# Attention with an MLP gate on one core: matmul sums in the mixer's second stage, first token transposes ahead of K and V, and a drain with a PSUM bank for each piece of Wo

## Chip, cores and metric

The kernel runs on one core of a Trainium2 chip. The metric is the device time of one execution in microseconds (us), the median of several runs. The profile is that of one execution, and its times are microseconds from the first instruction of the program.

## What is computed

```python
x = A_x                       # 2048 tokens, D = 512
xn = _layernorm(x)
# A: attention over a cache; 32 heads of 128, 2048 keys and values each
q = (xn @ wq) as 32 heads
p = softmax(q @ k_cache^T * 128 ** -0.5)
s = (p @ v_cache) @ wo
# B: a mixer and an MLP on the same xn
h  = gelu(_layernorm(xn) @ w1)                 # 512 -> 512
hs = (four column groups of h, shifted by +1, -1, +2, -2 tokens) @ w2
x1 = xn + hs
h2 = gelu(_layernorm(x1) @ w3) @ w4            # 512 -> 1792 -> 512
g = silu(x1 + h2)
return x + s * g
```

All inputs and the output are bf16.

## The kernel before

The attention is cut into 128 units. A unit is one head and one block of 512 queries; units run over 8 groups of 4 heads, in each group over 4 query blocks, and in each block over the 4 heads. A unit has 8 slots (`SPU`), and slot `n` of the whole program is unit `n // 8`, place `p = n % 8`. In a slot TensorE makes two score matmuls (keys by queries, 128x512 each) into a tile of two PSUM banks (`ps_s`, two buffers), and ScalarE turns them with one Exp into half of a `pT` tile. The value matmuls of a slot (`pv_slot`) run some slots after its scores; that distance is `lag`, 5 at first, up to 10 through most of the program, and 5 again at its end. The list `LAGS` says from which slot on which lag holds.

The denominators of a unit's softmax come from adding its four `pT` tiles on DVE (`add_first`, `add_next`) into `acc`, folding `acc` twice (`fold`), and summing over the 128 key partitions. For the last step there are two forms. In the first (`sums`) four matmuls of one column against a vector of ones write a [128, 4] tile in PSUM. In the second (`acc_turn`, `turned_sums`) a DMA transpose on SP's queue turns `acc`, and DVE reduces the turned tile along its free dimension. `turned(u)` chooses: units from `T0` up to `T1` use the second form. Either way DVE takes the reciprocals (`recip`), a DMA writes them to DRAM (`dr`), another one reads them back to all partitions (`rb`, in `bcast`), and DVE multiplies the unit's output by them (`norm`) on its way out of PSUM into `oT`. Unit `u` has these steps in the slots of the units after it:

| step | matmul sums | turned sums |
|---|---|---|
| last add, `fold` | unit u+1, places 0, 0 | unit u+1, places 0, 2 |
| sum over partitions | u+1, place 3 | u+1, place 3 (turn), u+2, place 0 (reduce) |
| `bcast` | u+1, place 4 | u+2, place 2 |
| `norm` | u+2, place 2 | u+2, place 7 |

The queries of unit `u + 2` are computed in places 0 and 1 of unit `u` (`q_mm`) and copied to SBUF in place 2 (`q_copy`), by DVE or by ScalarE. The product with Wo of a finished query block is made in places 4 and 5, one tile of 128 tokens for each unit (`wo_mm`), and added to `s_acc` in place 6 (`wo_post`). PSUM has eight banks: four for `ps_s`, two for the outputs `ps_o`, and one each for the tags `xa` (queries, sums, Wo) and `xm` (mixer and MLP).

The mixer and the MLP are cut into 136 chunks, and a planner lays them evenly over the units from the fifth to the 120th, at places 2, 3 and 6, 7. The chunks of the mixer's first matmul with its Gelu come first (units 5 to 18), those of its second one next (units 18 to 31, `m2_chunk`: a normalisation, a sum out of PSUM and token statistics on DVE for each), and those of the MLP after that. `w3_prefetch` loads the MLP's weights on GpSimd's queue.

Other work hangs on slots through `at(n, ...)`. `tokens` says in which slots the token tiles 4 to 15 get their statistics, their normalisation and their DMA transpose into `xnT` (on SP's queue); below it stand the slots of the loads of K, V and Wo for the first group, on the same queue. Work of one slot is issued in the order in which it was put there. Tiles 0 to 3 are turned on TensorE at the very start (`first_tokens`), since the first unit waits for them.

After the last slot comes the drain (L849 to L896): the value matmuls and sums of the last unit, then the product with Wo for the last four token tiles (`ts`, tiles 12 to 15). Each of these is the sum of a part for the last but one head group (`GL - 1`, held back) and one for the last group (`GL`). `last_scale` multiplies it by half the gate in `gf`, `last_out` adds the rest (prepared in `s_acc`) and stores the tile.

`pin` keeps an engine's instructions in the order of the program. All matmuls are issued through the helper on L115.

Of the kernel before, what the change touches and what calls it, by code (L numbers as in the profile page):

```python
# [17 lines left out]
def kernel(  # L18
# [95 lines left out]
    def mm(out, lhsT, rhs, start, stop):  # L114
        pin(nc.tensor.matmul(out=out, lhsT=lhsT, rhs=rhs, start=start, stop=stop))  # L115
# [11 lines left out]
    NS = NU * SPU  # L127
    T0, T1 = 3 * HG, NU - 10
    M2 = (18, 31)
    LAGS = [((T0 - 2) * SPU + 4 * (i + 1), LAG + i) for i in range(5)] + [((T1 + 2) * SPU + 2, LAG + 5)]  # L130
    LAGS += [((T1 + 2) * SPU + 6 + 4 * i, LAG + 4 - i) for i in range(4)] + [(NS, LAG)]
# [48 lines left out]
    def q_copy(u):  # L180
        qT = qtp.tile([P, 512], BF16, name="qT")
        if u > QUIET + 1 or M2[0] <= u - 2 <= M2[1]:
            pin(nc.scalar.activation(out=qT[:], in_=st[u].pop("psq")[:], func=ACT.Identity))
        else:
            pin(nc.vector.tensor_copy(out=qT[:], in_=st[u].pop("psq")[:]))  # L185
        st[u]["qT"] = qT
# [111 lines left out]

    def wo_part(ps, g, t, hhs, first, last):
        oT = oTs[(g, t // 4)]  # L300
        ts = t % 4
        for hh in hhs:
            mm(ps, oT[:, hh, ts * P:(ts + 1) * P], wos[g * HG + hh][:],
               first and hh == hhs[0], last and hh == hhs[-1])
# [22 lines left out]

    def last_scale(t, ps):
        gf, xf = tl[t]
        pin(nc.vector.scalar_tensor_tensor(  # L330
            out=gf[:], in0=ps, scalar=0.5, in1=gf[:], op0=ALU.mult, op1=ALU.mult))

    def last_out(t, eng):
        gf, xf = tl.pop(t)
        pin(eng.tensor_tensor(out=xf[:], in0=gf[:], in1=s_acc[:, t, :], op=ALU.add))
        pin(nc.sync.dma_start(out=out2d[t * P:(t + 1) * P, :], in_=xf[:]))

# [88 lines left out]
    def first_tokens():  # L426
# [18 lines left out]

        def back(t, eng, cs=slice(0, DC)):
            dst, src = xnT[:, cs, t * P:(t + 1) * P], tps[t][:, cs, :]
            if eng == "V":
# [8 lines left out]

        lo, hi = slice(0, DC // 2), slice(DC // 2, DC)
        turn(0)
# [6 lines left out]
        turn(3)  # L466
        for t in (2, 3):
            back(t, "A", lo)
            back(t, "V", hi)
        pin(nc.scalar.activation(out=qT[:, 0:2 * P], in_=qA[:, 0:2 * P], func=ACT.Identity))  # L470
# [255 lines left out]
    for t, (stats, apply, turn) in enumerate(tokens, 4):  # L726
# [4 lines left out]
        at(turn, lambda t=t: ln1_turn(t))  # L731
    for n, h, piece in ((2, 2, 2), (4, 2, 3), (12, 3, 0), (15, 3, 1), (19, 3, 2), (20, 3, 3)):
        at(n, lambda h=h, piece=piece: load_k(h, (piece,)))
    for n, h, half in ((7, 2, 0), (13, 2, 1), (20, 3, 0), (21, 3, 1)):
        at(n, lambda h=h, half=half: load_v(h, (half,)))
    at(28, ph1_load)
    at(64, w2_load)
    for h in range(HG):
        at(31 + h, lambda h=h: load_wo(h))
    for g in range(NG - 1):  # L740
# [137 lines left out]
    pc = psX.tile([P, D], FP32, tag="xa", name="ps_wo")  # L878
    dst = [pa[:, 0, :], pa[:, 1, :], pb[:, 0, :], pc[:]]
    for j in (0, 1):  # L880
        wo_part(dst[j], GL - 1, ts[j], held, True, False)
        wo_part(dst[j], GL, ts[j], ready, False, False)
    for j in (2, 3):
        wo_part(dst[j], GL - 1, ts[j], held, True, False)
    norm(U, 2)
    for j in (0, 1):
        wo_part(dst[j], GL, ts[j], (HG - 1,), False, True)
    for j in (2, 3):
        wo_part(dst[j], GL, ts[j], range(HG), False, True)
    for j in range(4):  # L890
        last_scale(ts[j], dst[j])
        if j < 2:
            last_out(ts[j], nc.gpsimd)
    for j in (2, 3):
        last_out(ts[j], nc.vector)
    ph.close()  # L896
# [30 lines left out]
```

## Time and profile before

| what | value |
|---|---|
| median of three runs | 1271.95 us (1271.66 to 1273.48) |
| the profiled execution | 1272.68 us |
| its span, first to last instruction | 1270.9 us |
| granted TensorE clock, mean | 0.999 |
| TensorE matmuls busy | 1254.7 us (99%) |
| DVE, ScalarE busy | 1099.7 us (87%), 1118.5 us (88%) |

The profile names its engines PE (TensorE matmuls), PEld (TensorE weight loads), DVE (VectorE), ACT (ScalarE), POOL (GpSimd) and SP (SyncE, which issues DMAs; SPq is its queue). In a timeline a row has its start, its length, engine, source line and operation, output and inputs, and how many instructions it merges; idle time of the engine before it stands in brackets with what ended it. In a table of groups the bar is followed by busy time and mean nanoseconds, and then by the idle time before the group. In a table of stretches each engine has its busy time and its count; the last three numbers are the granted clock, the DMA engines' busy share and GB/s. Matmuls are pipelined: a row's length includes a part that the next matmul overlaps.

### The profile page before, as it was taken

The numbers are of one execution on the slowest core, as the hardware profiler recorded it, in microseconds if no ns is written. First come the engines' busy times: TensorE is split into PE (matmuls) and PEld (weight loads), VectorE is DVE, ScalarE is ACT, GpSimd is POOL, SyncE is SP. The second block draws the span as 40 slices with busy tenths as digits, with TensorE's granted clock in tenths as the row PEclk, the third lists the DMA queues.
The fourth block names the chain that finished last, engine by engine and source line by source line (L and its number), as shares of the span: only waits on it lengthen the run. The fifth ranks groups of instructions, "written<-read, shape, count | busy, mean of one in ns | idle before, by whom it ended". The sixth has DMA issues, their size and how long they took to land.

```text
span 1270.9 us, 16580 instructions
## 1 busy us (share of the span) xinstructions
PE 1254.7 (99%) x5896; PEld 598.5 (47%) x5896; DVE 1099.7 (87%) x1499; ACT 1118.5 (88%) x1215; POOL 140.8 (11%) x239
## 2 busy tenths in 40 slices
PE   9999999999999999999999999999999999999998
PEld 5444444444444444444444444444444444444444
DVE  7888889998899888888898888989888899888886
ACT  8899998887999988899998889998888999988893
POOL 4420003333110010000000000000000000000111
PEclk9999999999999999999999999999999999999999
DMA  9533354466744465244454344435545344463532
GB/s 178 142 88 72 60 111 99 101 141 117 133 96 95 109 116 109 54 90 103 89 111 84 78 98 98 104 66 96 105 93 110 63 81 87 102 127 50 152 78 67
DMA packets 230612, 125.65 MB, mean 99 GB/s; under 512 B 182464, under 2 KB 207552, under 8 KB 230528
## 3 DMA queue, kind: packets, MB, share of 16 engines
q1 hardware_dynamic: 221568, 99.41, 39.9%
q0 software_dynamic: 8672, 24.91, 8.2%
q8 instruction: 46, 0.75, 0.3%
q14 instruction: 38, 0.31, 0.1%
q10 hardware_dynamic: 288, 0.26, 0.1%
HBM read 82.58 MB, written 7.60 MB: 71 GB/s over the span
## 4 chain that ended last, share of the span: by engine, by line
PE 70%; ACT 12%; DVE 11%; DMA 4%; issue 2%; POOL 0%; SPq 0%; DVEq 0%; POOLq 0%
PE ps_s L115 26%; PE ps_o L115 25%; ACT pT L199 9%; PE ps_m L115 7%; PE ps_wo L115 6%; PE ps_q L115 6%; DVE acc L210 4%; ACT pre L515 1%; DVE oT L279 1%; DMA rb<-dr 1%; ACT sq L485 1%; DVE sm L252 1%; ACT sq L494 1%; DVE acc L214 1%; DMA dr<-rc 1%
## 5 line engine op out<-in xcount | busy, mean ns | idle before, releaser
L199 ACT ACTIVATE pT<-ps_s 128x1024 bf16<-128x1024 f32 x1024 | 1013.5, 1033 | 129.5 <-PE ps_s L115 121.7
L115 PE MATMUL ps_s<-qT,kT 128*128 128x512 bf16 x2048 | 608.5, 379 | 2.8 <-ACT pT L199 0.8
L115 PE MATMUL ps_o<-pT,vb 128*128 128x512 bf16 x2048 | 607.7, 379 | 2.2 <-DVE oT L279 1.9
L115 PEld LDWEIGHTS <-kT 128*128 128x128 bf16 x2048 | 230.7, 113 | 237.4 <-issue 24.7
L210 DVE TENSOR_TENSOR acc<-acc,pT 128x2048 bf16<-128x2048 bf16 x254 | 307.1, 1209 | 18.1 <-ACT pT L199 17.1
L115 PEld LDWEIGHTS <-vb 128*128 128x128 bf16 x2048 | 199.6, 98 | 228.0 <-issue 3.3
L205 DVE TENSOR_TENSOR acc<-pT 128x2048 bf16<-128x2048 bf16 x128 | 156.1, 1219 | 24.0 <-ACT pT L199 23.4
L115 PE MATMUL ps_q<-xnT,wq_h 128*128 128x512 bf16 (+1 forms) x524 | 152.3, 374 | 2.5 <-DVE s_acc L353 1.1
L115 PE MATMUL ps_wo<-wo_h,oT 128*128 128x512 bf16 x468 | 138.9, 379 | 0.3 <-DVE rc L237 0.3
L279 DVE TENSOR_TENSOR oT<-ps_o,rb 128x512 bf16<-128x512 f32 x106 | 113.7, 1073 | 8.9 <-DMA rb<-dr 8.9
L353 DVE TENSOR_TENSOR s_acc<-ps_wo,s_acc 128x512 f32<-128x512 f32 x100 | 68.9, 689 | 52.5 <-PE ps_wo L115 52.4
L214 DVE TENSOR_TENSOR acc<-acc 128x1024 bf16<-128x1024 bf16 x127 | 87.0, 685 | 1.2
L185 DVE CAST qT<-ps_q 128x512 bf16<-128x512 f32 x108 | 74.1, 686 | 14.5 <-PE ps_q L115 14.5
L115 PEld LDWEIGHTS <-wq_h 128*128 128x128 bf16 x524 | 50.7, 98 | 63.6 <-issue 2.8
L252 DVE TENSOR_REDUCE sm<-accT 128x4 f32<-128x512 bf16 x106 | 72.2, 681 | 2.8 <-DMA accT<-acc 2.8
L115 PEld LDWEIGHTS <-oT 128*128 128x128 bf16 x480 | 46.9, 98 | 57.4 <-issue 1.1
L115 PE MATMUL ps_m<-xn2T,w_sb 128*128 128x512 bf16 x224 | 66.6, 379 | 0.0
L115 PE MATMUL ps_m<-w_sb,h2T 128*128 128x512 bf16 x224 | 64.0, 379 | 0.0
L640 POOL DMA_DIRECT2D w_sb<-in_B_w_dram x28 | 21.2, 758 | 361.8 <-PE ps_m L115 327.0
L215 DVE TENSOR_TENSOR acc<-acc 128x512 bf16<-128x512 bf16 x127 | 54.0, 425 | 4.4
L489 DVE SCALAR_TENSOR_TENSOR sq<-sq,pre 128x1024 bf16<-128x1024 bf16 x36 | 43.9, 1219 | 0.0
L515 ACT ACTIVATE pre<-ps_m 128x512 bf16<-128x512 f32 x72 | 42.7, 593 | 1.1 <-PE ps_m L115 1.1
(89 smaller groups left out, 559.2 us busy)
## 6 DMA issues: line engine op xcount, KB each, us to landing
rb<-dr SPq DMA_DIRECT2D x128, 256.0 KB, 4.2
vb<-in_A_v_cache_dram SPq DMA_DIRECT2D x64, 256.0 KB, 3.5
w_sb<-in_B_w_dram POOLq DMA_DIRECT2D x28, 256.0 KB, 4.3
wo_h<-in_A_wo_dram SPq DMA_DIRECT2D x32, 128.0 KB, 3.2
wq_h<-in_A_wq_dram SPq DMA_DIRECT2D x28, 128.0 KB, 3.1
kT<-in_A_k_cache_dram SPq DMA_TRANSPOSE x128, 3.5
dr<-rc SPq DMA_DIRECT2D x128, 2.0 KB, 1.6
xr<-in_A_x_dram POOLq DMA_DIRECT2D x16, 128.0 KB, 2.7
```

The source lines that it names most:

```text
L115: pin(nc.tensor.matmul(out=out, lhsT=lhsT, rhs=rhs, start=start, stop=stop))
L185: pin(nc.vector.tensor_copy(out=qT[:], in_=st[u].pop("psq")[:]))
L199: pin(nc.scalar.activation(out=s["pT"][-1][:, jj:jj + 2, :], in_=sps[:], func=ACT.Exp, scale=SCALE))
L205: pin(nc.vector.tensor_tensor(out=s["acc"][:], in0=s["pT"][0][:], in1=s["pT"][1][:], op=ALU.add))
L210: pin(nc.vector.tensor_tensor(out=a[:], in0=a[:], in1=st[u]["pT"][i][:], op=ALU.add))
L214: pin(nc.vector.tensor_tensor(out=a[:, 0:2, :], in0=a[:, 0:2, :], in1=a[:, 2:4, :], op=ALU.add))
L215: pin(nc.vector.tensor_tensor(out=a[:, 0, :], in0=a[:, 0, :], in1=a[:, 1, :], op=ALU.add))
L252: pin(nc.vector.tensor_reduce(out=sm[:], in_=s.pop("at")[:], axis=mybir.AxisListType.X, op=ALU.add))
L279: pin(nc.vector.tensor_tensor(out=oTs[(g, qt)][:, hh, :].rearrange(f, j=4), in0=s["o"].rearrange(f, j=4), in1=s["rb"].rearrange("x (p j) - ...
L353: pin(nc.vector.tensor_tensor(out=sa, in0=ps[:], in1=sa, op=ALU.add))
L489: pin(nc.vector.scalar_tensor_tensor(out=sq[:].rearrange(f2), in0=sq[:].rearrange(f2), scalar=1.0, in1=pre[:].rearrange(f2), op0=ALU.add, ...
L515: pin(nc.scalar.activation(out=pre[:, j, :], in_=mlp["ps"][:], func=ACT.Identity))
```

## The change

There are three parts. (1) `T0` goes from 12 to 32, so units 12 to 31 take matmul sums in place of turned ones; the slots at which the lag rises move with it, to start in unit 32 in place of unit 10; and the queries of units 20 to 33 are copied by DVE again, not by ScalarE. (2) In the loads for the first group, pieces of K of the fourth head (and one half of V of the third) and the Wo tiles move to later slots, which puts the transposes of token tiles 6 and 7 ahead of them; in `first_tokens` tiles 2 and 3 are each copied whole by one engine. (3) In the drain, the first three token tiles get a PSUM tile of their own each, and each is scaled and put out as soon as its last matmul is issued. The fourth one is cut into two halves of 256 columns, each with its own PSUM bank, its own matmuls for both head groups, its own scaling, add and store, the second store on ScalarE's queue.

```diff
-    T0, T1 = 3 * HG, NU - 10
-    M2 = (18, 31)
-    LAGS = [((T0 - 2) * SPU + 4 * (i + 1), LAG + i) for i in range(5)] + [((T1 + 2) * SPU + 2, LAG + 5)]
+    T0, T1 = 8 * HG, NU - 10
+    LAGS = [(T0 * SPU + 4 * (i + 1), LAG + i) for i in range(5)] + [((T1 + 2) * SPU + 2, LAG + 5)]
...
-        if u > QUIET + 1 or M2[0] <= u - 2 <= M2[1]:
+        if u > QUIET + 1:
             pin(nc.scalar.activation(out=qT[:], in_=st[u].pop("psq")[:], func=ACT.Identity))
...
-    def wo_part(ps, g, t, hhs, first, last):
+    def wo_part(ps, g, t, hhs, first, last, cs=slice(0, D)):
...
-            mm(ps, oT[:, hh, ts * P:(ts + 1) * P], wos[g * HG + hh][:],
+            mm(ps, oT[:, hh, ts * P:(ts + 1) * P], wos[g * HG + hh][:, cs],
...
-    def last_scale(t, ps):
+    def last_scale(t, ps, cs=slice(0, D)):
         gf, xf = tl[t]
         pin(nc.vector.scalar_tensor_tensor(
-            out=gf[:], in0=ps, scalar=0.5, in1=gf[:], op0=ALU.mult, op1=ALU.mult))
-
-    def last_out(t, eng):
-        gf, xf = tl.pop(t)
-        pin(eng.tensor_tensor(out=xf[:], in0=gf[:], in1=s_acc[:, t, :], op=ALU.add))
-        pin(nc.sync.dma_start(out=out2d[t * P:(t + 1) * P, :], in_=xf[:]))
+            out=gf[:, cs], in0=ps, scalar=0.5, in1=gf[:, cs], op0=ALU.mult, op1=ALU.mult))
+
+    def last_out(t, eng, cs=slice(0, D), queue=nc.sync):
+        gf, xf = tl[t]
+        pin(eng.tensor_tensor(out=xf[:, cs], in0=gf[:, cs], in1=s_acc[:, t, cs], op=ALU.add))
+        pin(queue.dma_start(out=out2d[t * P:(t + 1) * P, cs], in_=xf[:, cs]))
...
-        def back(t, eng, cs=slice(0, DC)):
-            dst, src = xnT[:, cs, t * P:(t + 1) * P], tps[t][:, cs, :]
+        def back(t, eng):
+            dst, src = xnT[:, :, t * P:(t + 1) * P], tps[t]
...
-        for t in (2, 3):
-            back(t, "A", lo)
-            back(t, "V", hi)
+        back(2, "A")
+        back(3, "V")
...
-    for n, h, piece in ((2, 2, 2), (4, 2, 3), (12, 3, 0), (15, 3, 1), (19, 3, 2), (20, 3, 3)):
+    for n, h, piece in ((2, 2, 2), (4, 2, 3), (15, 3, 0), (16, 3, 1), (19, 3, 2), (20, 3, 3)):
         at(n, lambda h=h, piece=piece: load_k(h, (piece,)))
-    for n, h, half in ((7, 2, 0), (13, 2, 1), (20, 3, 0), (21, 3, 1)):
+    for n, h, half in ((7, 2, 0), (15, 2, 1), (20, 3, 0), (21, 3, 1)):
         at(n, lambda h=h, half=half: load_v(h, (half,)))
...
-        at(31 + h, lambda h=h: load_wo(h))
+        at((34, 35, 37, 38)[h], lambda h=h: load_wo(h))
...
-    dst = [pa[:, 0, :], pa[:, 1, :], pb[:, 0, :], pc[:]]
+    dst = [pa[:, 0, :], pb[:, 0, :], pc[:]]
+    halves = [psX.tile([P, D], FP32, tag="xm", name="ps_wo"), psO.tile([P, D], FP32, tag="ps_o", name="ps_wo")]
     for j in (0, 1):
         wo_part(dst[j], GL - 1, ts[j], held, True, False)
         wo_part(dst[j], GL, ts[j], ready, False, False)
-    for j in (2, 3):
-        wo_part(dst[j], GL - 1, ts[j], held, True, False)
+    wo_part(dst[2], GL - 1, ts[2], held, True, False)
     norm(U, 2)
     for j in (0, 1):
         wo_part(dst[j], GL, ts[j], (HG - 1,), False, True)
-    for j in (2, 3):
-        wo_part(dst[j], GL, ts[j], range(HG), False, True)
-    for j in range(4):
         last_scale(ts[j], dst[j])
-        if j < 2:
-            last_out(ts[j], nc.gpsimd)
-    for j in (2, 3):
-        last_out(ts[j], nc.vector)
+        last_out(ts[j], nc.gpsimd)
+    wo_part(dst[2], GL, ts[2], range(HG), False, True)
+    last_scale(ts[2], dst[2])
+    last_out(ts[2], nc.vector)
+    for i, queue in enumerate((nc.sync, nc.scalar)):
+        cs = slice(i * D // 2, (i + 1) * D // 2)
+        ps = halves[i][:, cs]
+        wo_part(ps, GL - 1, ts[3], held, True, False, cs)
+        wo_part(ps, GL, ts[3], range(HG), False, True, cs)
+        last_scale(ts[3], ps, cs)
+        last_out(ts[3], nc.vector, cs, queue)
```

More of the change, by code (lines that the diff above doesn't have):

```diff
@@ L456, in q_part @@
                 mm(psq[:, ts], wqs[0][:, dc, :], xnT[:, dc, ts], dc == 0, dc == DC - 1)
-        lo, hi = slice(0, DC // 2), slice(DC // 2, DC)
         turn(0)
```

## The prediction

> **What bounds the kernel now.** I read the page first, then stretches of the span cut at the first score matmul of a unit (one head of one query block: 8 slots, each with two score matmuls, one Exp and two value matmuls).
>
> ```profile
> span 1270.9 us, 16580 instructions
> PE 1254.7 (99%) x5896; PEld 598.5 (47%) x5896; DVE 1099.7 (87%) x1499; ACT 1118.5 (88%) x1215; POOL 140.8 (11%) x239
> ```
>
> TensorE is busy nearly always, so a change pays only where it removes TensorE work or a place where TensorE stands still. The stretches show where that is:
>
> ```profile
> 82.86:92.70 9.84, 9.84 (x50) 4.69 (x48) 8.24 (x13) 9.84 (x13) 2.74 (x4) 1.00 0.60 153
> 102.54:131.67 29.13, 28.29 (x140) 13.42 (x138) 24.67 (x32) 27.73 (x31) 0.00 (x0) 1.00 0.43 74
> 131.67:141.44 9.77, 9.71 (x46) 4.56 (x45) 7.44 (x9) 9.77 (x13) 0.00 (x0) 1.00 0.22 48
> 190.09:319.71 129.62, 126.62 (x581) 59.86 (x580) 119.25 (x186) 109.20 (x118) 44.94 (x77) 1.00 0.53 115
> 277.99:287.57 9.58, 9.58 (x45) 4.53 (x44) 8.78 (x14) 8.36 (x10) 5.13 (x8) 1.00 0.78 182
> 287.57:298.24 10.67, 9.66 (x46) 4.54 (x45) 5.38 (x9) 8.58 (x10) 1.45 (x3) 1.00 0.63 112
> 298.24:310.06 11.82, 9.86 (x46) 4.55 (x44) 11.51 (x19) 8.06 (x10) 6.17 (x10) 1.00 0.71 127
> ```
>
> Columns: stretch, length, then busy time and count of PE, weight loads, DVE, ACT, POOL. The lines are unit 8 (matmul sums, lag 5), units 10 to 12 (lag going from 5 to 10), unit 13 (turned sums, lag 10), units 19 to 31 (the mixer's second stage), and of these units 28, 29 and 30. Units 28, 29 and 30 have the same matmuls, yet 29 is 1.09 us and 30 is 2.24 us longer than 28. That is 3.3 us of standing TensorE in the stretch that the change rewrites. What stood in the way:
>
> ```profile
> 286.25 1.67 POOL L640 DMA_DIRECT2D w_sb<-in_B_w_dram  x2
> 286.46 0.34 SPq L269 DMA_DIRECT2D rb<-dr  x1
> 286.90 1.22 SPq L247 DMA_TRANSPOSE accT<-acc  x1
> 290.65 1.05 DVE L279 TENSOR_TENSOR oT<-ps_o,rb 128x512 bf16<-128x512 f32 x1 [2.19 <-DMA rb<-dr]
> 294.55 0.69 DVE L252 TENSOR_REDUCE sm<-accT 128x4 f32<-128x512 bf16 x1 [2.84 <-DMA accT<-acc]
> 300.33 0.59 PE L115 MATMUL ps_q<-xnT,wq_h 128*128 128x512 bf16 x2 [1.07 <-DVE s_acc L353]
> 303.55 0.59 PE L115 MATMUL ps_o<-pT,vb 128*128 128x512 bf16 x2 [0.89 <-DVE oT L279]
> ```
>
> Two loads of 256 KB for the MLP start on POOL at 286.25; the turn of `acc` issued at 286.90 is read only at 294.55, 7.6 us later. DVE waits 2.84 us for it, all behind it on DVE is late, and TensorE then waits for DVE twice.
>
> **Part 1, matmul sums for units 12 to 31.** It removes 20 DMA turns and 20 reduces, so the wait at 294.55 has nothing left to wait for: **-3.3 us**. Kept from below: if DVE comes just as late through `rb`, nothing is won (rival B). It adds 20 times four one-column matmuls. Their price:
>
> ```profile
> 1247.88 0.27 PE L115 MATMUL ps_sum<-ones_t,acc 128*128 128x1 bf16 x4
> 1248.01 0.60 PE L115 MATMUL ps_s<-qT,kT 128*128 128x512 bf16 x2
> ```
>
> The next score pair starts 0.13 us after the sums. Unit 8 against unit 13 gives 0.07 (ScalarE has its say in that stage). I take 0.13 for the 15 units from 17 on and 0.07 for five: **+2.3 us**, bounds 1.4 to 2.6.
>
> On DVE:
>
> ```profile
> L210 DVE TENSOR_TENSOR acc<-acc,pT 128x2048 bf16<-128x2048 bf16 x27 | 32.6, 1207 | 0.6 <-ACT pT L199 0.6
> L568 DVE SCALAR_TENSOR_TENSOR xr<-ps_m,xr 128x512 bf16<-128x512 f32 x16 | 11.0, 687 | 1.5 <-PE ps_m L115 1.0
> L214 DVE TENSOR_TENSOR acc<-acc 128x1024 bf16<-128x1024 bf16 x13 | 9.0, 692 | 0.4
> L252 DVE TENSOR_REDUCE sm<-accT 128x4 f32<-128x512 bf16 x13 | 8.9, 683 | 2.8 <-DMA accT<-acc 2.8
> L215 DVE TENSOR_TENSOR acc<-acc 128x512 bf16<-128x512 bf16 x13 | 5.5, 425 | 0.4
> L183 ACT ACTIVATE qT<-ps_q 128x512 bf16<-128x512 f32 x13 | 7.7, 592 | 0.0
> ```
>
> ```profile
> L279 DVE TENSOR_TENSOR oT<-ps_o,rb 128x512 bf16<-128x512 f32 x106 | 113.7, 1073 | 8.9 <-DMA rb<-dr 8.9
> L185 DVE CAST qT<-ps_q 128x512 bf16<-128x512 f32 x108 | 74.1, 686 | 14.5 <-PE ps_q L115 14.5
> L286 DVE TENSOR_TENSOR oT<-ps_o,rb 128x512 bf16<-128x512 f32 x21 | 14.4, 684 | 4.1 <-DMA rb<-dr 4.1
> ```
>
> Per unit DVE loses a reduce (0.68) and the slow form of the normalisation (1.07 becomes 0.68), and in 14 units takes over the q copy (0.69) from ScalarE (0.59). Net -0.4 us per unit, from 119.25 busy in 129.62 us, so DVE has a little more room. ScalarE gets more too. Units 19 to 31 hold 580 wide matmuls. What one costs from start to start comes from the page:
>
> ```profile
> L115 PE MATMUL ps_s<-qT,kT 128*128 128x512 bf16 x2048 | 608.5, 379 | 2.8 <-ACT pT L199 0.8
> ```
>
> They run in 1024 pairs of 0.594 us (608.5 over 1024), and the second alone takes 0.379, so it starts 0.215 after the first; with the rounding, 0.216. 580 of them are 125.3 of the 129.62 us, 3.3 of the rest are the stall above, and 1.0 is small waits. With ScalarE lighter I take off two thirds: **-0.7 us**, bounds -1.0 and 0.
>
> The new wait: TensorE, in order, may not pass the sums at slot 3 before DVE has folded `acc` and copied q out of the same PSUM tag. Behind it stand all score and value matmuls. From unit start to the sums are three slots of 1.22 us and a fourth's matmuls (0.87): 4.5 us. DVE, in the worst order, does in that time an L568 left over from slot 7 (0.69), the last add (1.21), both folds (0.69 and 0.43) and the copy (0.69): 3.7 us. So 0.8 us is spare when DVE enters the unit on time; where two mixer chunks fall in one unit it may not. I allow **+0.4 us** in all, bounds 0 and 3 (beyond that is rival A).
>
> The rise of the lag from 5 to 10 moves from units 10 to 12 to units 32 to 34. Ten value matmuls are put off there (2.2 us), but ScalarE can't follow: the line counts 126 wide matmuls beside 12 sums and two that reach in from outside, so with the ten there would be 136, which is three units like unit 8 and four matmuls, 30.4 us. Less 2.2 that is 28.2, and the line says 29.13, so the rise costs 0.9 us. Units 32 to 34 open the MLP's Gelu stage with a like load on ScalarE: I take the same there, **0**, bounds -0.9 and +1.0.
>
> **Part 2, transposes of tokens 6 and 7 ahead of pieces of K and V.**
>
> ```profile
> 26.01 1.15 SPq L151 DMA_TRANSPOSE kT<-in_A_k_cache_dram  x1
> 28.51 0.58 SPq L161 DMA_DIRECT2D vb<-in_A_v_cache_dram  x1
> 29.19 1.20 SPq L419 DMA_TRANSPOSE xnT<-xn  x1
> 33.49 0.61 PE L115 MATMUL ps_q<-xnT,wq_h 128*128 128x512 bf16 x2 [0.92 <-DMA xnT<-xn]
> 57.42 0.27 PE L115 MATMUL ps_sum<-ones_t,acc 128*128 128x1 bf16 x4 [0.98 <-DVE qT L185]
> ```
>
> SP issues in order. A piece of K (1.15) and one of V (0.58) go ahead of the transpose that TensorE waits for; moved behind, that transpose is issued about 1.8 us earlier, and the transfers it no longer follows are out of its way. The wait (0.92, about 1.1 from start to start) goes: **-1.1 us**, with -1.5 as the other bound if `rb` of unit 0 gains as well. Late next would be that piece of K. It is issued near 28.5, and the transpose issued at 29.19 ended TensorE's wait at 33.49, 4.3 us on, so the piece lands near 33. Unit 3 wants it: two slots after the q matmuls (four score, two value and two q matmuls, 1.7 us), which then come at 32.4, so near 34.1. That cover is about 1 us; if it is gone, the gain is 0. The Wo loads move behind a 2 KB and a 256 KB transfer; the wait at 57.42 is for DVE: **0**.
>
> **Part 3, the first tokens.**
>
> ```profile
> 8.89 0.87 DVE L449 CAST xnT<-ps_s 128x256 bf16<-128x256 f32 x2 [0.48 <-ACT xnT L451]
> ```
>
> DVE's two halves waited 0.48 for ScalarE's half of the same PSUM tile and end at 9.76. A whole copy from 8.9 takes 0.69 (L185), so it ends at 9.6, and then four small matmuls follow instead of two. **0**, bounds -0.2 and +0.2.
>
> **Part 4, the drain.**
>
> ```profile
> 1263.77 1.89 DVE L330 SCALAR_TENSOR_TENSOR gf<-ps_s,gf 128x512 bf16<-128x512 f32 x3 [1.42 <-PE ps_s L115]
> 1264.43 1.03 PE L115 MATMUL ps_wo<-wo_h,oT 128*128 128x512 bf16 x4
> 1264.55 2.27 POOL L335 TENSOR_TENSOR xf<-gf,s_acc 128x512 bf16<-128x512 bf16 x2 [20.26 <-DVE gf L330]
> 1265.73 2.60 SPq L336 DMA_DIRECT2D out_dram<-xf  x4
> 1266.17 1.80 DVE L335 TENSOR_TENSOR xf<-gf,s_acc 128x512 bf16<-128x512 bf16 x2
> ```
>
> TensorE's end stays: after the last normalisation it has 6 wide and 16 half matmuls (1.3 and 1.7 us) for 10 wide ones (2.2), but starts them 0.9 earlier. DVE sets the end. Today its first scaling starts at 1263.77, since two pieces share a tile; apart, it starts near 1262.7. Three scalings at 0.6 end near 1264.6, and the add of piece 2 comes next, while POOL does its two (2.27, to about 1265.7). Today's pair of adds took 1.80, with the first beside POOL, where alone each takes about 0.6; so I let this add end 0.55 after POOL, at 1266.3. Four half-width steps at 0.35 end at 1267.7, where today's last add ends at 1267.97. With the last transfer half as big: **-0.4 us**, bounds -1.2 (no clash with POOL) and +1.0 (half-width steps at full price).
>
> A rule speaks against this change: the Trainium skill, page "TensorE: Matmul & The Clock Gate", section on packing small matmuls, lets a weight load overlap a running matmul only when their row groups differ. All of ours use all rows, so each load would be paid in full (rival D). The trace disagrees: 1254.7 us of matmuls and 598.5 of loads fit in 1270.9.
>
> **Sum.** -3.3 + 2.3 - 0.7 + 0.4 + 0 - 1.1 + 0 - 0.4 = -2.8 us. The profiled execution took 1272.68 us (span 1270.9 and 1.8 around it), 0.7 above the median of 1271.95. So 1269.9 by its clock, and 1269.1 as a median. A difference under 0.2% (2.5 us) is about what a measurement of this kernel can't tell from none.
>
> **Rivals.** A, slower: DVE is later than the 0.8 us spare in the second stage, and TensorE stands before the sums. For it: the row at 57.42, where just that cost 0.98 us. Against: units with matmul sums and mixer work already run, unit 8 with all its 9.84 us busy. From 0.2 us a unit on (2.8 over 14) it eats the gain; at half the wait of 57.42, 0.5 us in 14 units, it adds 7, 0.4 of which the sum has: 1275.7. B, no change: the stall of 3.3 us stays, since `rb` shares the transfers with the MLP loads as the turn did. For it: 2.19 us of waiting for `rb` at 290.65. Against: that `rb` was issued at 286.46, after the first load had started, and was there 4.2 us on, and the new order, as the old one, has seven slots from reciprocal to normalisation. It gives 1272.4. C: the reordering at the start only moves the wait from the transposes to K, whose cover is the 1 us above: 1270.2. D, by the page's rule: 80 and 16 more loads at 0.10 each (598.5 over 5896) would add 9.7 in place of 2.3: 1276.5.
>
> **How the numbers follow.** Forecast 0.60, A 0.15, B 0.14, C 0.10, D 0.01. The forecast's own range, 1266.4 to 1270.8, has three quarters of its chance (0.46) below 1269.4, since more of its bounds lie below the sum than above; C adds 0.02, so faster is 0.48. The rest of the forecast (0.14), B and the rest of C (0.08) lie within 0.2%: 0.36. A and D make 0.16 slower. The range for 8 in 10 goes from 1265.4 (small waits, `rb` and drain at their good ends) to 1273.4, which takes in C, B and A where it is mild.
>
> **What would show it.** Right: no wait for `accT` near 294, units 29 and 30 at about 9.7 us; units 19 to 31 near 127.8 us in all (129.62 - 3.3 - 0.7 + 1.8 for sums, + 0.4); the wait for `xnT` near 33 gone; last add ending 0.2 to 0.7 before today's against the last matmul. Wrong: TensorE waits before `ps_sum` for DVE in many of units 18 to 31 (A), waits of the normalisation for `rb` near 290 (B), a score matmul waiting for K near 34 (C).

## The result and the profile after

The changed kernel takes 1269.97 us (median of 20 runs, 1268.74 to 1271.52), the kernel before, run beside it, 1272.49 us (20 runs, 1271.46 to 1276.95). The ratio is 0.9978, with an interval of 0.9972 to 0.9985: 2.5 us or 0.2% less, where -2.8 us was forecast. The profiled execution took 1270.0 us, 2.7 less than that of before.

The page of the changed kernel, its span, its busy times and the slow form of the normalisation:

```profile
span 1268.2 us, 16717 instructions
PE 1256.0 (99%) x5984; PEld 602.0 (47%) x5984; DVE 1091.5 (86%) x1494; ACT 1112.5 (88%) x1200; POOL 140.9 (11%) x239
L278 DVE TENSOR_TENSOR oT<-ps_o,rb 128x512 bf16<-128x512 f32 x86 | 92.2, 1073 | 1.0 <-DMA rb<-dr 1.0
```

TensorE has more to do (1256.0 for 1254.7 us) in a shorter span, so what went was standing time. DVE's waiting for `rb` ahead of this group fell from 8.9 to 1.0 us. Stretches of the changed kernel, cut as before at the first score matmul of a unit: units 10 to 12, 19 to 31, and of these 28, 29 and 30; then 32 to 34:

```profile
102.09:132.10 30.01, 29.96 (x149) 14.41 (x148) 24.85 (x32) 27.90 (x31) 0.00 (x0) 1.00 0.38 73
191.63:318.83 127.20, 127.20 (x633) 61.71 (x632) 115.23 (x186) 103.79 (x105) 45.83 (x78) 1.00 0.46 108
280.25:289.88 9.63, 9.63 (x49) 4.68 (x48) 8.34 (x13) 8.00 (x9) 5.63 (x9) 1.00 0.84 153
289.88:299.51 9.63, 9.63 (x50) 4.68 (x48) 8.34 (x13) 8.00 (x9) 2.83 (x4) 1.00 0.50 124
299.51:309.17 9.66, 9.66 (x49) 4.68 (x48) 8.65 (x16) 7.57 (x9) 4.69 (x9) 1.00 0.52 128
318.83:347.11 28.28, 27.78 (x131) 13.19 (x130) 23.15 (x30) 26.75 (x30) 3.15 (x6) 1.00 0.58 130
```

Units 28, 29 and 30 are now alike, at 9.63 to 9.66 us, and TensorE is busy in all of units 19 to 31. They take 127.20 us for 129.62. DVE's normalisation in unit 29, which stood 2.19 us before, starts without a wait (timeline of the changed kernel):

```profile
293.61 0.68 DVE L285 TENSOR_TENSOR oT<-ps_o,rb 128x512 bf16<-128x512 f32 x1
```

The view of one tile, `ps_sum`, shows who TensorE waited for ahead of the sums, in the whole program, as us and times:

```profile
  DVE qT L184: 1.3, 2
```

Both waits lie at the start (0.18 and 1.14 us, the second one shown below); none is in units 12 to 31.

The sum form also normalises a unit earlier, so a query block's product with Wo moves one unit forward. In unit 17 it comes in (9.6 us for 8.7 before), in unit 37 it goes out (9.6 for 10.4), and the two nearly cancel. Stretches of the changed kernel for `ps_wo` alone, those two units, PE and DVE:

```profile
172.17:181.78 9.61, 1.19 (x4) 0.69 (x1) 1.00 0.62 94
366.64:376.21 9.57, 0.00 (x0) 0.00 (x0) 1.00 0.32 89
```

At the start (timeline of the changed kernel), both turns of tokens 6 and 7 are issued at 25.68, ahead of the pieces of K and V, and TensorE waits for no `xnT` near 33. Later waits grew, though:

```profile
25.68 2.52 SPq L418 DMA_TRANSPOSE xnT<-xn  x2
40.52 0.61 PE L115 MATMUL ps_o<-pT,vb 128*128 128x512 bf16 x2 [0.42 <-DMA vb<-in_A_v_cache_dram]
47.99 0.69 DVE L285 TENSOR_TENSOR oT<-ps_o,rb 128x512 bf16<-128x512 f32 x1 [1.36 <-DMA rb<-dr]
56.98 0.27 PE L115 MATMUL ps_sum<-ones_t,acc 128*128 128x1 bf16 x4 [1.14 <-DVE qT L184]
```

The drain of the changed kernel (timeline):

```profile
1259.19 0.76 DVE L285 TENSOR_TENSOR oT<-ps_o,rb 128x256 bf16<-128x256 f32 x2 [0.28 <-DMA rb<-dr]
1260.10 1.29 DVE L329 SCALAR_TENSOR_TENSOR gf<-ps_s,gf 128x512 bf16<-128x512 f32 x2 [0.15 <-PE ps_s L115]
1260.88 2.28 POOL L334 TENSOR_TENSOR xf<-gf,s_acc 128x512 bf16<-128x512 bf16 x2 [18.46 <-DVE gf L329]
1262.02 1.68 DVE L334 TENSOR_TENSOR xf<-gf,s_acc 128x512 bf16<-128x512 bf16 x1
1264.86 0.43 DVE L334 TENSOR_TENSOR xf<-gf,s_acc 128x256 bf16<-128x256 bf16 x1
```

From the start of the last normalisation to the end of the last add are 6.10 us, for 6.37 before (1261.60 to 1267.97); to the landing of the last store 7.70, for 8.12. Here the normalisation itself started late, by a wait of 0.28 us for `rb`. In the traces of `e3_ends_alone` and `e13_changed_again` (both below), where it didn't wait, the two distances are 6.28 and 7.88, and 6.28 and 7.87: of the gain, 0.1 and 0.2 us are the drain's own.

Put together, between the two profiled executions: start +0.1, units 2 to 5 -0.5, units 10 to 59 -2.6, unit 117 +0.3, unit 127 with the drain +0.1 (its `rb` landed later, which ate the drain's gain); all else within 0.1. That is the 2.7 us of the two spans.

### The profile page after: what moved, and what is told of

The parts are those of the page before. It is cut to its first block, busy times and chain, and to the rows that moved or that the text cites. A ratio compares the mean times of both kernels' runs of the same rounds, so it can differ in the third digit from the quotient of the medians.

```text
span 1268.2 us, 16717 instructions
## 1 busy us (share of the span) xinstructions
PE 1256.0 (99%) x5984; PEld 602.0 (47%) x5984; DVE 1091.5 (86%) x1494; ACT 1112.5 (88%) x1200; POOL 140.9 (11%) x239
## 4 chain that ended last, share of the span: by engine, by line
PE 78%; ACT 12%; DVE 7%; issue 2%; DMA 1%; POOL 0%; SPq 0%; DVEq 0%; ACTq 0%
PE ps_s L115 29%; PE ps_o L115 27%; ACT pT L198 9%; PE ps_m L115 8%; PE ps_wo L115 7%; PE ps_q L115 7%; DVE acc L209 2%; ACT pre L512 1%; ACT sq L482 1%; DMA rb<-dr 1%; ACT sq L491 1%; DVE oT L278 1%; DMA dr<-rc 1%; DVE acc L204 0%; PE ps_sum L115 0%
## 5 line engine op out<-in xcount | busy, mean ns | idle before, releaser
L115 PE MATMUL ps_wo<-wo_h,oT 128*128 128x512 bf16 (+1 forms) x476 | 140.2, 378 | 0.0
L184 DVE CAST qT<-ps_q 128x512 bf16<-128x512 f32 x122 | 83.7, 686 | 14.1 <-PE ps_q L115 14.0
L278 DVE TENSOR_TENSOR oT<-ps_o,rb 128x512 bf16<-128x512 f32 x86 | 92.2, 1073 | 1.0 <-DMA rb<-dr 1.0
L251 DVE TENSOR_REDUCE sm<-accT 128x4 f32<-128x512 bf16 x86 | 58.6, 681 | 0.1
L669 POOL DMA_DIRECT2D g_d<-xr x16 | 8.8, 547 | 319.5 <-DVE xr L667 319.5
```

The source lines that it names most:

```text
L251: pin(nc.vector.tensor_reduce(out=sm[:], in_=s.pop("at")[:], axis=mybir.AxisListType.X, op=ALU.add))
L278: pin(nc.vector.tensor_tensor(out=oTs[(g, qt)][:, hh, :].rearrange(f, j=4), in0=s["o"].rearrange(f, j=4), in1=s["rb"].rearrange("x (p j) - ...
```

## The experiments

In all edits below a line with a minus is of the kernel named, and the line with a plus takes its place; three dots stand for lines left out. A run is also named by its number alone (`e4`). Units are cut at their first score matmul. Eight of the traces lack 116 or 118 of their matmul records (the three parts alone, `e4`, `e7`, `e11`, `e12` and `e13`); where the text cuts units there, the lengths are good to 0.1 us.

**The parts alone.** Three kernels take one part of the change each into the kernel before.

`e1_sums_alone`: the two hunks of part 1 (`T0`, `LAGS`, `q_copy`) and nothing else.

```diff
-    T0, T1 = 3 * HG, NU - 10
+    T0, T1 = 8 * HG, NU - 10
...
```

> The kernel before with part 1 alone: matmul sums for units 12 to 31, the lag raised in units 32 to 34, q copies of units 20 to 33 on DVE. If the whole gain is this part (my theory: the turned sum at units 28 to 30 waits behind two MLP loads), the stretch from unit 10 to unit 34 shrinks by 2.6 us as in the changed kernel, units 29 and 30 take about 9.65 us each, start and drain stay to within 0.1 us, and the median falls by 2.3 to 3 us. If the parts need each other (a stall comes back without the other two), it falls by less than 1.5 us.

Measured: 1268.64 us against 1271.10 for the kernel before (ratio 0.9985, interval 0.9975 to 0.9995). Units 29 and 30:

```profile
289.32:308.72 19.40, 19.35 (x97) 9.48 (x97) 17.11 (x29) 15.69 (x17) 7.64 (x13) 1.00 0.48 127
```

They took 22.49 before (10.67 + 11.82). Part 1 alone gains as much as the whole change, within the noise.

`e2_loads_alone`: the moved loads of the first group and nothing else.

```diff
-    for n, h, piece in ((2, 2, 2), (4, 2, 3), (12, 3, 0), (15, 3, 1), (19, 3, 2), (20, 3, 3)):
+    for n, h, piece in ((2, 2, 2), (4, 2, 3), (15, 3, 0), (16, 3, 1), (19, 3, 2), (20, 3, 3)):
...
```

> The kernel before with the moved loads and transposes of the first group alone (first tokens, sums and drain as before). Theory: the wait for the token transposes in unit 2 (1.1 us) goes, but about half comes back in units 3 to 5, where value matmuls wait for a half of V and the sums wait for DVE: unit 6 starts 0.4 to 0.7 us earlier than in the kernel before. Rival: the half comes back only because the first tokens start 0.1 us later in the changed kernel; then unit 6 starts 1.0 us or more earlier. The stall in units 29 and 30 stays at about 3.3 us in both cases; median 0.3 to 1 us lower.

Measured: 1270.43 us, ratio 0.9998 (0.9986 to 1.0009): nothing that can be measured. Unit 2 takes 8.09 us, as in every trace with the new order; with the old order it takes 9.0 to 9.7 (9.56 in the profile before). Units 3 to 5 give part of that back. Units 2 to 5 together take 35.3 to 37.0 us in the seven traces with the new order and 36.1 to 37.5 in the seven with the old one, so half a microsecond is less than what executions of one kernel differ by there. The stall in units 29 and 30 is there, 23.66 us in this trace.

`e3_ends_alone`: the whole copies in `first_tokens` and the new drain, nothing else.

> The kernel before with the two ends alone: first tokens 2 and 3 copied whole by one engine each, and the drain with a bank for each piece. Theory: neither brings anything; first score matmul 0.1 us later (near 10.55) and last unit 26.6 to 26.75 us long against 26.6, since DVE's add of piece 2 waits for GpSimd's second add. Median within 0.6 us of before. If the drain's 0.1 us of loss in the changed kernel came only from a late normalisation there, the last unit is 0.2 to 0.4 us shorter here.

Measured: 1270.98 us, ratio 0.9999 (0.9988 to 1.0009). From the last normalisation to the last landing are 7.88 us, between the 8.12 of before and the 7.70 of the change; a gain of some tenths is below what the times tell.

**Is it the MLP loads?** `e4_prefetch_spread`: the kernel before, with the two MLP weight loads apart, one hook earlier and one later, so that they don't start together at 286.25.

```diff
-        if t == 12:
-            hooks[len(chunks)] = lambda n: [w3_prefetch() for _ in range(2)]
+        if t in (11, 14):
+            hooks[len(chunks)] = lambda n: w3_prefetch()
```

> The kernel before, with turned sums throughout the second stage as it had, but the two first loads of MLP weights, which it issues together in unit 28, issued one at a time, three chunks apart (before the 12th and the 15th chunk of the second stage). Theory (two loads at once hold up the turn of acc by 7.6 us): the wait of DVE for accT near 294 shrinks to under 0.5 us and units 29 and 30 together take at most 20.2 us in place of 22.5; median 2 to 3 us lower. Rival (DVE, 92% busy there with turned sums, falls behind by itself, or SP's queue does): the stall stays above 2.5 us in all, there or in a neighbouring unit.

Measured: 1270.65 us, ratio 0.9992 (0.9981 to 1.0003): nothing that can be measured. In the trace the loads start at 277.99 and 301.46, and most of the stall stays: units 29 and 30 take 21.83. But it is not where it was. The two units, one by one, as stretches:

```profile
287.08:299.25 12.17, 9.60 (x44) 4.54 (x44) 8.25 (x13) 8.56 (x10) 2.82 (x4) 1.00 0.52 96
299.25:308.79 9.54, 9.49 (x45) 4.56 (x44) 9.23 (x17) 7.96 (x10) 5.16 (x9) 1.00 0.64 144
```

Unit 30, which took 11.82 us before, has no stall left; unit 29, 10.67 before, is longer. The timeline:

```profile
282.15 0.58 SPq L166 DMA_DIRECT2D wq_h<-in_A_wq_dram  x1
282.83 0.61 SPq L239 DMA_DIRECT2D dr<-rc  x1
287.30 0.34 SPq L269 DMA_DIRECT2D rb<-dr  x1
291.68 1.05 DVE L279 TENSOR_TENSOR oT<-ps_o,rb 128x512 bf16<-128x512 f32 x1 [3.68 <-DMA rb<-dr]
292.64 0.68 DVE L252 TENSOR_REDUCE sm<-accT 128x4 f32<-128x512 bf16 x1
292.78 0.59 PE L115 MATMUL ps_o<-pT,vb 128*128 128x512 bf16 x2 [2.52 <-DVE oT L279]
```

The turn of `acc` now lands 4.9 us after its issue, for 7.6 before, and DVE's reduction at 292.64 doesn't wait for it, where it waited 2.84. So the MLP loads did hold up the turn, as the prediction said, and the stall of unit 30 went with them. They are not the cause of the rest. In the kernel before, too, TensorE's first wait in this place (timeline) was not for the turn but for a normalisation that had waited 2.19 for `rb`:

```profile
291.76 0.59 PE L115 MATMUL ps_o<-pT,vb 128*128 128x512 bf16 x2 [1.01 <-DVE oT L279]
```

In `e4_prefetch_spread` that wait for `rb` is 3.68. The transfer of `rb` is not slow (4.4 us, for a median of 4.2 of all 128 on the page of before); its issue is late, 4.5 us after that of `dr`, for whose landing it waits. The edit is no clean removal, either: one MLP load now starts at 277.99, just ahead of the loads for the next head group, and `dr` takes 4.5 us where it took 3.4. So the question is what makes a 2 KB write so late. SP's queue in the kernel before, in the same place (timeline):

```profile
278.66 1.25 SPq L151 DMA_TRANSPOSE kT<-in_A_k_cache_dram  x1
280.00 0.53 SPq L166 DMA_DIRECT2D wq_h<-in_A_wq_dram  x1
280.59 0.50 SPq L161 DMA_DIRECT2D vb<-in_A_v_cache_dram  x1
281.14 1.14 SPq L151 DMA_TRANSPOSE kT<-in_A_k_cache_dram  x1
282.33 0.57 SPq L166 DMA_DIRECT2D wq_h<-in_A_wq_dram  x1
283.00 0.45 SPq L239 DMA_DIRECT2D dr<-rc  x1
```

Five loads for the next head group go out in 4.2 us, and `dr` right behind them. The view of DMA issues for 276 to 292 gives its time from issue to landing (count, size, median us):

```profile
dr<-rc SPq DMA_DIRECT2D x1, 2.0 KB, 3.4
```

The median of all 128 on the page of before:

```profile
dr<-rc SPq DMA_DIRECT2D x128, 2.0 KB, 1.6
```

SP stands until `dr` has landed before it issues `rb` (286.46), and the turn of the next unit's `acc` stands behind `rb` (286.90), late enough to meet the MLP loads. Theory two, then: the first that is late is `dr`, held up by the group's loads in front of it on SP's queue; it makes `rb` late, and the turn. The rival is that only the turned form itself, with its longer chain over SP, is at fault.

`e10_wq_later`: the kernel before, turned sums and all; in this one group the two Wq loads of the burst go from unit 27 to unit 30.

```diff
-            at((b + (-4, -4, -1, -1)[hh]) * SPU + (5, 7)[hh % 2], lambda h=h: load_w(h))
+            at((b + ((-4, -4, 2, 2) if g == 1 else (-4, -4, -1, -1))[hh]) * SPU + (5, 7)[hh % 2], lambda h=h: load_w(h))
```

> The kernel before, with two Wq loads of the next group moved from unit 27 to unit 30, out of SP's queue ahead of the reciprocals of unit 26. Theory (SP's order and the transfers behind it make rb late): the reciprocals go out about 1.1 us sooner, DVE's wait for rb in unit 29 shrinks by 0.8 us or more, and units 29 and 30 take at most 21.5 us together. Rival (only the three legs by DMA, each some 4 us here, are too long): they stay between 21.8 and 23.7 us as in the kernels with turned sums so far.

Measured: 1267.96 us (one run). SP's queue (timeline) and units 29 and 30 (stretch):

```profile
276.57 1.34 SPq L151 DMA_TRANSPOSE kT<-in_A_k_cache_dram  x1
277.96 0.57 SPq L161 DMA_DIRECT2D vb<-in_A_v_cache_dram  x1
278.57 1.15 SPq L151 DMA_TRANSPOSE kT<-in_A_k_cache_dram  x1
279.82 0.52 SPq L239 DMA_DIRECT2D dr<-rc  x1
281.76 0.32 SPq L269 DMA_DIRECT2D rb<-dr  x1
282.18 1.22 SPq L247 DMA_TRANSPOSE accT<-acc  x1
```

```profile
286.39:305.52 19.13, 19.13 (x90) 9.12 (x89) 17.85 (x29) 16.32 (x19) 7.80 (x14) 1.00 0.57 130
```

With three loads ahead in place of five, `rb` follows `dr` after 1.9 us in place of 3.5 and the turn is issued at place 4 of unit 28 (276.81 on), where it was at place 7. That is ahead of the MLP loads, which start at 284.44 here, and the turn lands after 4.0 us. In units 28 to 30 DVE waits for neither, and the stall is gone with turned sums still in place. Two loads moved by three units do in this stage what 20 units of matmul sums did. The Trainium skill, page "DMA: Bandwidth & Descriptors", section on queues, rings and completion order, says that a transfer's semaphore write lands only after every earlier write of the same DMA engine. That agrees with a `dr` of 2 KB that takes 3.4 us behind five loads and 1.6 in the median. It lands 0.55 us after the second Wq load, the last to land of all transfers issued ahead of it; in the other 13 traces, 0.16 to 0.99 us after the last of these.

`e11_wq_later_timed`, the same kernel with times:

> The kernel before with the two Wq loads moved from unit 27 to unit 30 again, now timed. Theory (the order on SP's queue alone made the stall, and turned sums were no fault): median 2.5 to 4 us below the kernel before, at or a little below the changed kernel timed beside it. Rival (the one look met a lucky run): less than 1.5 us below.

Measured: 1267.98 us (11 runs) against 1270.90; ratio 0.9983 (0.9972 to 0.9994). Units 29 and 30 take 19.24. In this trace `dr` still takes 2.9 us, but it is issued 4.2 us into unit 28 in place of 5.0, and the turn (285.29) goes out 0.9 us ahead of the MLP loads (286.23) and lands after 4.0. No kernel takes the MLP loads from beside the turn and leaves `dr` as it was, so how the 3.3 us divide between the two causes is not measured exactly.

**What the sum form costs.** `e9_sums_24_31`: the kernel before with matmul sums in units 24 to 31 alone, turned ones on both sides; the queries stay with ScalarE.

```diff
     def turned(u):
-        return T0 <= u < T1
+        return T0 <= u < T1 and not 24 <= u < 32
...
```

(The steps of `bcast` and `normed` at the seam of the two forms are placed as at `T1`.)

> The kernel before, with matmul sums in units 24 to 31 alone; units 12 to 23 keep turned sums, the lag rises in units 10 to 12 and ScalarE copies the queries as before. New theory: with turned sums the reciprocals reach SP's queue a transfer later, lateness adds up in the units where the next group's K, V and Wq are loaded, and a row in units 29 and 30 stops; only the form of the sum there matters. Then units 29 and 30 take 19.2 to 19.5 us together (22.5 before), each of the eight units pays about 0.13 us, and the median falls by 1.5 to 2.5 us. Rival (the gain comes with the later rise of the lag or with the copies on DVE): units 29 and 30 stay above 21.5 us.

Measured: 1270.73 us, ratio 1.0001 (0.9990 to 1.0013): the fall of 1.5 to 2.5 us did not come. Units 29 and 30 fall to 19.80, but units 25, 27 and 28 are 0.5 longer each. Timeline of this kernel, one of the waits:

```profile
272.47 0.27 PE L115 MATMUL ps_sum<-ones_t,acc 128*128 128x1 bf16 x4 [0.31 <-ACT qT L183]
```

The sums wait for the query copy out of their PSUM tag. With that copy on ScalarE this is rival A on another engine, and with the price of the sums it eats the gain. In the changed kernel, with the copies on DVE, units 25, 27 and 28 take 9.63 to 9.66 us, for 10.04 to 10.10 here; so the third edit of part 1, the copies on DVE, is needed for the first.

`e5_lag_early`: the changed kernel, with the lag rising in units 10 to 12 again.

```diff
-    LAGS = [(T0 * SPU + 4 * (i + 1), LAG + i) for i in range(5)] + [((T1 + 2) * SPU + 2, LAG + 5)]
+    LAGS = [(10 * SPU + 4 * (i + 1), LAG + i) for i in range(5)] + [((T1 + 2) * SPU + 2, LAG + 5)]
```

> The changed kernel with the lag rising in units 10 to 12 as before the change, and matmul sums to unit 31. Theory (place of the rise is worth nothing): units 10 to 34 together take as long as in the changed kernel (235.0 us) to within 0.4 us; units 10 to 12 get 0.9 us shorter and units 32 to 34 as much longer. Rival (lag 5 in the second stage is part of the gain): stalls come back in units 29 and 30, 1 us or more.

Measured: 1269.77 us (one run). Units 10 to 59 as one stretch, in the kernel before, in the changed one, in this one and in `e10_wq_later`:

```profile
102.54:595.53 492.99, 488.40 (x2247) 231.07 (x2246) 436.28 (x593) 442.17 (x481) 67.47 (x114) 1.00 0.50 100
```

```profile
102.09:592.51 490.42, 489.32 (x2327) 233.74 (x2326) 426.79 (x587) 436.51 (x467) 67.54 (x114) 1.00 0.46 95
```

```profile
101.37:592.43 491.06, 489.60 (x2328) 233.92 (x2327) 426.64 (x587) 436.94 (x467) 68.06 (x114) 1.00 0.44 95
```

```profile
101.36:590.85 489.49, 487.89 (x2248) 231.09 (x2247) 436.47 (x593) 441.70 (x481) 67.21 (x114) 1.00 0.50 101
```

These four lines take part 1 apart. Curing the stall alone is worth 492.99 - 489.49 = 3.5 us in these traces (2.9 by the times of `e11_wq_later_timed`). The 20 units of sums and DVE copies, with the lag where it was and no stall on either side, cost 491.06 - 489.49 = 1.6. The later rise of the lag gives back 491.06 - 490.42 = 0.6, where it was expected to be worth nothing. The stretch repeats well where no stall is in it: 489.49 to 489.50 in `e10`, `e11` and `e12`, 490.42 to 490.70 in the five traces that have part 1 as it is in the change. With the stall it varies, 492.58 and 494.12 in `e3` and `e2`. The 491.06 is of one trace.

**The drain.** `e8_scales_first`: the changed kernel; DVE does its five scalings first and its three adds after them.

```diff
     last_scale(ts[2], dst[2])
-    last_out(ts[2], nc.vector)
...
         last_scale(ts[3], ps, cs)
+    last_out(ts[2], nc.vector)
+    for cs, queue in zip(cuts, (nc.sync, nc.scalar)):
         last_out(ts[3], nc.vector, cs, queue)
```

> The changed kernel with DVE's order in the drain altered: all five scalings out of PSUM first, then the three adds. Theory (the add of piece 2 stood 1.1 us because GpSimd's second add held the port they share): from the last normalisation to DVE's last add 5.2 to 5.4 us in place of 6.10, with the add of piece 2 ending 0.55 us after GpSimd's second one. Rival (that add is slow by itself, and no port is shared): it takes 1.1 us or more again with GpSimd done, and the end moves by less than 0.3 us.

Measured: 1268.83 us (one run); 5.61 us from the last normalisation to the last add, for 6.10 in the changed kernel's profile and 6.28 in `e13_changed_again`, and not quite the 5.2 to 5.4 expected. Timeline:

```profile
1260.11 2.28 POOL L334 TENSOR_TENSOR xf<-gf,s_acc 128x512 bf16<-128x512 bf16 x2 [18.44 <-DVE gf L329]
1260.53 1.17 DVE L329 SCALAR_TENSOR_TENSOR gf<-ps_wo,gf 128x512 bf16<-128x512 f32 x2
1262.15 0.42 DVE L329 SCALAR_TENSOR_TENSOR gf<-ps_wo,gf 128x256 bf16<-128x256 f32 x1 [0.45 <-PE ps_wo L115]
1262.49 1.35 DVE L334 TENSOR_TENSOR xf<-gf,s_acc 128x512 bf16<-128x512 bf16 x3
```

While GpSimd adds, DVE's scalings out of PSUM go on at their usual pace (0.68 for one of 512 columns, 0.68 to 0.69 for those ahead of it). All three of its adds behind GpSimd's take 1.35 together, where one that began beside GpSimd's took 1.68 (the row at 1262.02 above). DVE now waits for TensorE (0.45) before its last scaling.

**The start.** `e7_v_early`: the changed kernel, with the first half of V of the fourth head a slot earlier, ahead of the piece of K in slot 20.

```diff
-    for n, h, half in ((7, 2, 0), (15, 2, 1), (20, 3, 0), (21, 3, 1)):
+    for n, h, half in ((7, 2, 0), (15, 2, 1), (19, 3, 0), (21, 3, 1)):
```

> The changed kernel with the first half of V of the fourth head issued one slot earlier, ahead of the rb of unit 1, for whose dr SP waits. Theory (that half stands behind SP's wait, and value matmuls of unit 3 wait for it): no wait of ps_o for vb near 40 us, unit 3 back at about 8.4 us (8.87 in the changed kernel); units 2 to 5 together 36.2 to 36.6 us in place of 36.96. Rival (the transfers are too many, not their order): the wait moves to another piece, and units 2 to 5 stay within 0.2 us of 36.96.

Measured: 1268.09 us (one run); no wait for `vb`, and units 2 to 5 take 35.62 us for 36.96. `e13_changed_again` is the changed kernel itself, timed beside it:

> The changed kernel itself, timed beside the two above: 2 to 3 us below the kernel before (ratio 0.9978 when first measured).

Measured: 1268.88 us (11 runs), ratio 0.9984 (0.9975 to 0.9992), and units 2 to 5 without the edit:

```profile
25.42:60.75 35.33, 34.77 (x171) 16.80 (x173) 31.49 (x52) 31.89 (x34) 13.96 (x24) 1.00 0.67 153
```

The wait for `vb` was not there either. So `e7_v_early` says nothing: the waits of the start differ between executions by more than the edit can bring.

**A version that beats both.** `e12_best`: the kernel before with turned sums, lag, copies and first tokens as they were; the Wq loads of `e10_wq_later`; the moved loads of the change with V as in `e7_v_early` and the mixer's first weights at slot 33; and the drain of the change in the order of `e8_scales_first`.

> The kernel before with the two Wq loads moved as above, the moved loads of the first group with V a slot earlier and the mixer's first weights five slots later, and the drain with all scalings first; turned sums, lag and q copies as before the change. By the sum of the parts: 3.5 us from units 29 and 30, 0.5 to 1.1 from units 2 to 5, 0.5 to 0.7 from the drain, so 4.5 to 5.3 us below the kernel before and about 2 below the changed one.

Measured: 1265.63 us (5 runs, 1265.48 to 1266.45), ratio 0.9964 (0.9951 to 0.9978) against 1270.90; the changed kernel, timed beside it, took 1268.88. Units 29 and 30 take 19.24, units 2 to 5 35.25, and from the last normalisation to the last add are 5.61 us.

## Why the prediction was right, and where it was not

The time and the sign were right, -2.5 for -2.8. Step by step, by the profiled executions:

| step | forecast | measured |
|---|---|---|
| stall in units 29 and 30 | -3.3 | -3.5 (`e10_wq_later`) |
| sums, with small waits | +2.3 - 0.7 | +1.6 (`e5_lag_early` less `e10_wq_later`) |
| allowance for late DVE | +0.4 | 0 |
| later rise of the lag | 0 | -0.6 |
| moved loads | -1.1 | -0.5 here, nothing measurable alone |
| first tokens | 0 | +0.1, less than what executions differ by |
| drain | -0.4 | +0.1 for the whole last unit; -0.4 behind a normalisation that was itself late |
| not forecast: unit 117 | | +0.3 |

The terms miss by up to 0.6 us, and the misses cancel: stall, allowance and lag came out 1.2 us better than forecast, loads, first tokens, drain and unit 117 1.5 worse. That the total is within 0.3 is in part luck.

The stall. Its size and its end came as forecast; the reason given was half of it. The prediction saw two MLP loads of 256 KB start 0.65 us before the turn of `acc` and put the whole 3.3 us down to them. `e4_prefetch_spread` took them from beside the turn: the wait for the turn and the stall of unit 30 went, as that mechanism has it, but unit 29 stayed long. `e10_wq_later` left them and took two Wq loads out from in front of `dr`; `rb` was there in time, the turn went out ahead of the MLP loads, and both waits went. The step that failed is that nothing but the turn stood in the way: of the 3.3 us, the 1.09 of unit 29 come at 291.76, behind the wait of 2.19 for `rb`, before DVE gets to the turn, and the turn met the MLP loads only because `rb` stood ahead of it. The quoted rows began at 286.25; the burst that makes `dr` late is in the rows just above, from 278.66. The changed kernel does not cure the late `dr`: it is issued at 285.08 there and `rb` only at 288.89, 3.8 us later. It lives with it: no turn is left to be late, and the normalisation comes 8.5 us after the issue of `dr` (293.61, no wait), where in the kernel before DVE was ready for it 5.5 us after (288.46 and 283.00), since `dr` stood behind the burst.

The sums. The price of 0.13 us for four one-column matmuls and the two thirds off the small waits gave 1.6, and 1.6 it is; no run takes the two apart. The allowance was not needed: in the `ps_sum` view no wait lies in units 12 to 31, so the 0.8 us of spare on DVE was enough everywhere, and rival A did not happen. `e9_sums_24_31` shows that it would have with the copies on ScalarE. Units 19 to 31 took 127.20 us for the 127.8 forecast (13 units at 0.13 are 1.7, not the 1.8 of that sum). Rival D counted 96 more loads; there are 88 (5984 for 5896), as the drain adds 8 and not 16. Its price for them was not paid anywhere: part 1 as a whole gained 2.6. By the rule on which D rests (the Trainium skill, page "TensorE: Matmul & The Clock Gate", section on packing small matmuls) loads and matmuls of the same row groups don't overlap. The trace disagrees: 1256.0 us of matmuls and 602.0 of loads lie in 1268.2.

The lag. With 2.2 us of value matmuls put off, the rise shortens units 10 to 12 by only 0.9 us (30.01 without it in the changed kernel, 29.13 with it in `e5_lag_early`), so it costs 1.3 there, where the prediction had worked out 0.9 from unit 8. Units 32 to 34 it shortens by 1.5 (28.28, and 29.74 without it in `e5_lag_early`), so there it costs 0.7. "A like load on ScalarE" was the step that failed, by 0.6 us, within its bound of -0.9.

The loads. The wait for `xnT` went as said. What came of it was overrated: -1.5 us in unit 2, but +0.9 in units 3 to 5, where V came late (0.42), the normalisation waited longer for `rb` (1.36 for 0.98), DVE was late by that, and the sums at 56.98 waited 1.14. That is rival C's mechanism, a wait that only moves, at another place than it named: V and `rb` in place of K. As `e13_changed_again` shows, though, these waits are not there in every execution. The prediction took the wait at 57.42 for one on DVE that the loads don't reach; through `rb` they do. Rival B was wrong for the changed kernel, but its wait for `rb` is the one that `e4_prefetch_spread` shows.

The drain. The add of piece 2 was to end 0.55 us after GpSimd's; it ended 0.54 after (1263.70 and 1263.16). The half-width steps took 0.42 each in place of 0.35, and the first scaling began 0.9 us after the normalisation's start in place of 1.1; the two cancel, and the last add ends 0.27 earlier against the normalisation, as worked out. That is luck: in `e3_ends_alone` and `e13_changed_again` the first scaling begins 1.09 after the normalisation's start, as forecast, and the last add ends only 0.09 earlier. The step that failed is the price of the half-width steps.

Open: the 0.3 us of unit 117 come in each trace of the changed kernel and in none of the kernels with one part alone, and nothing was run to explain it. Whether two loads on another queue would hold up `dr` as well was not run. What sets the waits of the start from one execution to the next was not settled either.

## What to carry to other kernels

When a small transfer is late, read its queue backwards from its issue: here some 3 us were lost because loads issued up to 4 us ahead of it held it up, and moving two of them was worth at least as much as rewriting 20 units of compute. A forecast can have the size of a stall right and half of its cause wrong. A kernel that moves the suspect tells, if its trace is read wait by wait: the time of `e4_prefetch_spread` hardly moved, yet one of the two waits was gone. Look also at what the suspect is moved beside. Edits at a program's start, where many transfers are under way (the DMA engines were busy for 0.64 to 0.74 of units 2 to 5), need several executions or a good many runs before a gain of a microsecond can be believed.

## What the runs showed of the hardware

- A transfer of 2 KB took 3.4 us from issue to landing close behind five loads on its queue, 1.9 to 2.9 behind three (`e10`, `e11`, `e12`), and 1.6 us in the median of 128. In each of the 14 traces, the one in unit 28 landed 0.16 to 0.99 us after the last landing among the transfers issued ahead of it.
- A DMA transpose (the turn of `acc`) took 7.6 us with two loads of 256 KB starting around it, 4.9 without them (`e4`), and 3.5 to 4.0 when it was issued ahead of them (`e10`, `e11`, `e12`).
- DVE's add of two SBUF operands that starts beside GpSimd's took 1.68 us, ending 0.54 us after it; behind it, an add takes less than 0.7 (three in 1.35, two of them of half width). Scalings with one operand in PSUM were not slowed. The Trainium skill, page "GPSIMD Engine Reference", section on specifications, says that GpSimd shares its SBUF interfaces with VectorE and contends with instructions that have two SBUF inputs; this trace agrees, and it looks as if DVE waited until GpSimd is done: in the kernel before, an add that began later beside GpSimd's took 1.20 us and ended 0.55 after it.
- Four one-column matmuls with their weight loads cost about 0.08 us of a unit, net of the small waits that went with the turned form and ScalarE's copies (1.6 us over 20 units).
